# A gated conv and residual quantizer on one core: the first of two sums of conv taps by an accumulating DMA transfer, the second on DVE, and eight of 24 residual updates on DVE

## The chip, the cores and the metric

The kernel runs on one core of one Trainium2 chip. The metric is the device time of one execution in microseconds, lower is better. All runs quoted are of the same ("fast") state, and every comparison is with runs of the kernel before on the same chip in the same rounds.

A core has five engines that run side by side, each in its own instruction order: PE (matmuls), DVE (vector), ACT (scalar), GpSimd (called POOL in the profile) and SP (which here only issues DMA transfers). The order on each engine is fixed when the kernel is built: the scheduler that builds it takes the written program and reorders each engine's instructions within what the data dependences allow. At run time each engine works strictly through that order, so an instruction that waits holds up all those behind it on its engine.

## The reference, cut to what matters

`x` has 2 x 16000 positions of 512 channels (bf16).

```python
z = sum over the 3 taps of xp[:, i:i+T, :] * dw_enc[i]      # depthwise conv, each step rounded to bf16
z = silu(z)                                                 # the gate
res = z
for s in range(4):                                          # four codebooks of 8 entries
    idx = argmin over the 8 entries of the squared distance to res
    q, res = q + cb[idx], res - cb[idx]
y = the same kind of 3-tap conv on q
```

## The kernel before: the parts that matter

The positions are cut into 18 tiles of 1792 (128 rows of 14). For each tile:

- SP issues 14 transposing DMA loads into one of two input buffers `X` (channels on the partitions). GpSimd copies the two halo columns.
- DVE makes three products ("taps") of 128x1792 for each of 4 blocks of channels and adds them up in two rounded sums. ACT and DVE compute the gate from that.
- The quantizer makes chains of small dependent DVE instructions ("decisions": V, KEY, M, OHA and so on, 128x112 elements), each chain closed by PE. 24 residual updates follow: PE computes `pu` into PSUM (the memory that takes PE's results), and either ACT evicts it (after an identity matmul has added the old residual) or DVE adds it. Before, 18 are on ACT and 6 on DVE.
- PE decodes into `py`, ACT copies that to `Y`, and the result is stored.

The tiles overlap in a pipeline: the front of a tile (taps to gate) is worked between the quantizer steps of the tile ahead of it.

```python
def taps(st, i):                                   # once per block of channels, i = 0..3
    X = XT[st["n"] % NX]                           # NX = 2 input buffers
    pk = []
    for k in range(K):                             # three products
        t = ppool.tile([P, R], BF16, name=f"P{k}") # pools of 3 buffers each
        nc.vector.tensor_scalar(out=t, in0=X[:, i, k:k + G, :]..., scalar1=WENC[:, i, k:k + 1], ..., op0=ALU.mult)
        pk.append(t)
    nc.vector.tensor_tensor(out=pk[0], in0=pk[0], in1=pk[1], op=ALU.add)   # first rounded sum
    nc.vector.tensor_tensor(out=pk[0], in0=pk[0], in1=pk[2], op=ALU.add)   # second rounded sum
    nc.scalar.activation(pk[1], pk[0], ACT.Exp, scale=-1.0)

def update(st, s, i, u, on_act):
    ...                                            # PE: pu = [identity @ z if on_act] - codebook @ one-hot
    if on_act: nc.scalar.copy(zg, v)
    else:      nc.vector.tensor_tensor(out=zg, in0=zg, in1=v, op=ALU.add)
# in resid(): update(st, s, i, u, m % 4 != 3)      # m = 0..23
```

## Time and profile before

Time before: 887.77 us, the median of 3 runs (886.93 to 888.55).

| | kernel before |
|---|---|
| repeat of one tile in mid-run | 44.4 us |
| from the start to the first one-hot window copy (`OHW`, 96x896), the fill | 99.7 us |
| from the last such copy to the end, the tail | 50.1 us |
| DVE waits in all | 126 us |

The repeat is read as the distance between the 18 window copies, which come once a tile. The busy line of the page:

```profile
PE 631.2 (71%) x4660; PEld 358.7 (40%) x4711; DVE 739.6 (83%) x1526; ACT 736.1 (83%) x667; POOL 79.7 (9%) x143
```

The windows view, one stretch in mid-run (columns: stretch, its length, busy us of PE, PEld (PE's loading of weights), DVE, ACT and POOL, the clock granted to PE as a share of full speed, DMA share, GB/s):

```profile
500.00:545.00 45.00, 35.65 (x263) 20.01 (x264) 40.45 (x82) 41.19 (x38) 3.80 (x4) 0.92 0.41 84
```

DVE and ACT are both busy for some 40 of 44.4 us a tile. Neither is full, so I read the bound as a loop of DVE, ACT and PE and not as one engine; no run shows this alone, but experiment 6 fits it. What DVE waits for (us in total, times, longest):

```profile
DVE rr L288 <- PE pgr L270: 36.1, 21, 3.3
DVE ZB_139 L386 <- PE pu L380: 27.7, 21, 3.0
DVE ZB_138 L386 <- PE pu L380: 20.2, 19, 3.0
DVE ZB_137 L386 <- PE pu L380: 11.8, 16, 1.5
```

The three `ZB` lines (the updates, 60 us) and `rr` (a reduction of a PE result, 36 us) are all the larger waits of the steady state.

### The profile page before, as it was taken

Reading aid. Unit: us, or ns where it says so; the run is one execution under the profiler, and the core shown is the slowest. Engines: PE = TensorE matmul, PEld = TensorE weight load, DVE = VectorE, ACT = ScalarE, POOL = GpSimd, SP = SyncE. Lnnn points to the kernel's source line nnn. Section 1 sums busy time; section 2 is a strip of 40 time slices with the busy share of each in tenths; the row PEclk is TensorE's granted clock in tenths of the full one; section 3 lists DMA queues with packets and bytes.
Section 4 is the critical chain, followed back from the end, with each engine's and each line's share of the span. In section 5 each row is a group of like instructions: output and inputs, shape, how many; then the busy total and the mean of one; then the engine's idle time right before and its main releaser. Section 6 shows DMA issues by size and latency. Waiting matters only on the chain.

```text
span 888.2 us, 12372 instructions
## 1 busy us (share of the span) xinstructions
PE 631.2 (71%) x4660; PEld 358.7 (40%) x4711; DVE 739.6 (83%) x1526; ACT 736.1 (83%) x667; POOL 79.7 (9%) x143
## 2 busy tenths in 40 slices
PE   1003587878787877777878787878787878778892
PEld 0002253535353535353535353535353535444540
DVE  4499999898989898989898989898989898984731
ACT  0076797989898989898989898989898989997572
POOL 5000000101010101010101010101010100000000
PEclk9998698989898989898989898989898989999997
DMA  4412322343434343434343534333534342020213
GB/s 96 95 30 59 78 46 39 94 74 92 75 94 73 96 71 97 70 100 67 99 68 99 68 97 66 103 65 100 67 99 67 98 69 78 7 84 1 84 51 112
DMA packets 143021, 67.20 MB, mean 76 GB/s; under 512 B 139932, under 2 KB 140572, under 8 KB 140700
## 3 DMA queue, kind: packets, MB, share of 16 engines
q1 hardware_dynamic: 137088, 33.06, 21.7%
q0 software_dynamic: 3840, 32.77, 11.8%
q10 hardware_dynamic: 2032, 0.56, 0.3%
q8 instruction: 37, 0.61, 0.3%
q14 instruction: 24, 0.20, 0.1%
HBM read 0.56 MB, written 32.77 MB: 38 GB/s over the span
## 4 chain that ended last, share of the span: by engine, by line
DVE 39%; ACT 29%; PE 22%; issue 5%; SPq 3%; DMA 1%; ACTq 0%; POOL 0%; POOLq 0%; DVEq 0%
PE pu L380 9%; PE pu L379 7%; ACT ZB_139 L384 6%; ACT ZB_137 L384 5%; ACT Y L402 5%; ACT ZB_138 L384 5%; SPq L228 3%; DVE ZB_137 L255 2%; DVE ZB_138 L255 2%; DVE ZB_139 L255 2%; PE pgr L270 2%; PE py L397 2%; DVE M L324 1%; DVE ZB_138 L386 1%; DVE ZB_139 L386 1%
## 5 line engine op out<-in xcount | busy, mean ns | idle before, releaser
L402 ACT CAST Y<-py 128x1024 bf16<-128x1024 f32 x126 | 130.6, 1043 | 13.8 <-PE py L397 13.8
L384 ACT CAST ZB_138<-pu 128x896 bf16<-128x896 f32 x108 | 95.9, 932 | 18.5 <-PE pu L380 18.0
L384 ACT CAST ZB_139<-pu 128x896 bf16<-128x896 f32 x108 | 95.6, 933 | 17.2 <-PE pu L380 16.7
L384 ACT CAST ZB_137<-pu 128x896 bf16<-128x896 f32 x108 | 95.7, 935 | 10.5 <-PE pu L380 10.5
L379 PEld LDWEIGHTS <-IDENT 128*128 128x128 bf16 x648 | 65.6, 101 | 77.8 <-issue 18.9
L270 PE MATMUL pgr<-ZB_137 128*128 128x152 bf16 (+1 forms) x672 | 56.4, 232 | 50.7 <-DVE ZB_137 L255 47.7
L379 PE MATMUL pu<-ZB_137,IDENT 128*128 128x512 bf16 (+1 forms) x216 | 81.1, 375 | 9.3 <-ACT ZB_137 L384 8.2
L379 PE MATMUL pu<-ZB_138,IDENT 128*128 128x512 bf16 x216 | 80.6, 373 | 7.8 <-ACT ZB_138 L384 6.7
L379 PE MATMUL pu<-ZB_139,IDENT 128*128 128x512 bf16 x216 | 80.1, 371 | 8.3 <-ACT ZB_139 L384 7.0
L267 PE MATMUL pgr<-MSK,IDENT 128*128 128x456 bf16 (+3 forms) x180 | 61.0, 339 | 23.2 <-ACT ZB_137 L384 4.8
L270 PEld LDWEIGHTS <-ZB_137 128*128 128x128 bf16 x672 | 48.4, 101 | 70.3 <-DVE ZB_137 L255 52.3
L288 DVE TENSOR_REDUCE rr<-pgr 128x6 f32<-128x768 f32 (+1 forms) x54 | 41.9, 775 | 36.2 <-PE pgr L270 36.1
L425 POOL DMA_DIRECT2D out_dram<-Y x66 | 34.1, 521 | 389.6 <-ACT Y L402 389.3
L386 DVE TENSOR_TENSOR ZB_139<-ZB_139,pu 128x896 bf16<-128x896 bf16 x36 | 39.1, 1085 | 27.9 <-PE pu L380 27.7
L386 DVE TENSOR_TENSOR ZB_138<-ZB_138,pu 128x896 bf16<-128x896 bf16 x36 | 39.0, 1083 | 20.5 <-PE pu L380 20.2
L270 PE MATMUL pgr<-ZB_139 128*128 128x152 bf16 (+1 forms) x672 | 53.3, 226 | 3.0 <-ACT ZB_139 L384 2.9
L270 PE MATMUL pgr<-ZB_138 128*128 128x152 bf16 (+1 forms) x672 | 53.6, 226 | 2.5 <-ACT ZB_138 L384 2.5
L270 PEld LDWEIGHTS <-ZB_139 128*128 128x128 bf16 x672 | 46.6, 98 | 18.4 <-issue 9.1
L270 PEld LDWEIGHTS <-ZB_138 128*128 128x128 bf16 x672 | 46.6, 98 | 17.7 <-issue 8.9
L386 DVE TENSOR_TENSOR ZB_137<-ZB_137,pu 128x896 bf16<-128x896 bf16 x36 | 39.0, 1084 | 12.1 <-PE pu L380 11.8
L242 ACT ACTIVATE P_348<-P_346 128x1792 bf16<-128x1792 bf16 x1 | 1.7, 1696 | 43.6 <-DVE P_346 L241 43.6
L380 PEld LDWEIGHTS <-CBN_0_262 128*128 128x128 bf16 x144 | 18.9, 131 | 32.6 <-issue 25.3
(1280 smaller groups left out, 1741.0 us busy)
## 6 DMA issues: line engine op xcount, KB each, us to landing
out_dram<-Y POOLq DMA_DIRECT2D x18, 1568.0 KB, 8.5
out_dram<-Y POOLq DMA_DIRECT2D x14, 196.0 KB, 8.2
XT_164<-in_x_dram SPq DMA_TRANSPOSE x126
XT_165<-in_x_dram SPq DMA_TRANSPOSE x126
out_dram<-Y POOLq DMA_DIRECT2D x30, 12.0 KB, 2.1
out_dram<-Y POOLq DMA_DIRECT2D x2, 210.0 KB, 8.9
WDBC<-in_dw_dec_dram ACTq DMA_DIRECT2D x1, 384.0 KB
CB_94<-in_codebooks_dram ACTq DMA_DIRECT2D x16, 8.0 KB
```

The lines of the kernel that those rows point to most:

```text
L228: nc.sync.dma_start_transpose(out=X[:, :, g + 1, :], in_=src[g])
L255: nc.vector.tensor_tensor(out=Z[:, i, :, N3:N3 + P], in0=pk[0].rearrange("p (g c) -> p g c", c=P), in1=pk[1].rearrange("p (g c) -> p g c", ...
L267: nc.tensor.matmul(o, lhsT=IDENT, rhs=MSK[:, 0:nb, c0:c1], start=True, stop=False)
L270: nc.tensor.matmul(o[:, u * w:(u + 1) * w], lhsT=Z[:, i, b0 + u, N3:N3 + P], rhs=Z[:, i, b0 + u, c0:c1], start=False, stop=(u == nb - 1 an ...
L288: nc.vector.tensor_reduce(out=grp(st["rr"], g0, g1)[:, :, :, 0], in_=v[:, :, :, N3:N3 + P], axis=AX.X, op=ALU.max)
L379: nc.tensor.matmul(o, lhsT=IDENT, rhs=zg[:, k0:k0 + nk, :], start=True, stop=False)
L380: nc.tensor.matmul(o, lhsT=CBN[s, u][:, i * P:(i + 1) * P], rhs=W[:, k0:k0 + nk, PADC:PADC + P], start=not on_act, stop=True)
L384: nc.scalar.copy(zg, v)
L386: nc.vector.tensor_tensor(out=zg, in0=zg, in1=v, op=ALU.add)
L397: nc.tensor.matmul(o, lhsT=W[:, k, PADC:PADC + P], rhs=WDEC[u], start=True, stop=not wrap)
L402: nc.scalar.copy(Y[:, 2 * k:2 * k + 2, :].rearrange("p g d -> p (g d)"), py)
L425: nc.gpsimd.dma_start(out=view[p0:p1, lo:hi, :], in_=Y[p0:p1, lo:hi, :])
```

## The change

The intent is to relieve DVE and ACT, the two busiest engines. Half of the rounded sums (72 adds of 1.08 us) leave DVE for the DMA engines: the second product is added into the first by an accumulating transfer. In return DVE takes two more of the 24 updates of each tile from ACT. To make room for the latency, the front is split into steps with positions of their own (`LAG`, in tiles), the pools get their own depths (`NB`), and the stores move to SP and are cut in two. Setup buffers are freed early to make space.

```diff
+    BYDMA = (1,)
+    NB = (5, 3, 4, 3)                       # buffers of P0, P1, P2, E
+    LAG = (0.01, 0.16, 0.31, 0.41, 0.42, 0.60)
...
-            t = ppool.tile([P, R], BF16, name=f"P{k}")
+            t = ppool.tile([P, R], BF16, name=f"P{k}", bufs=NB[k])
...
-        nc.vector.tensor_tensor(out=pk[0], in0=pk[0], in1=pk[1], op=ALU.add)
-        nc.vector.tensor_tensor(out=pk[0], in0=pk[0], in1=pk[2], op=ALU.add)
-        nc.scalar.activation(pk[1], pk[0], ACT.Exp, scale=-1.0)
+    def add(st, i, k):
+        pk = st["pk", i]
+        if k in BYDMA:
+            nc.gpsimd.dma_start(out=pk[0], in_=pk[k], accum_op=ALU.add)
+        else:
+            nc.vector.tensor_tensor(out=pk[0], in0=pk[0], in1=pk[k], op=ALU.add)
+    # expo, plus1, inverse and gate become steps of their own, with a buffer E for the exponential
...
-            nc.gpsimd.dma_start(out=view[p0:p1, lo:hi, :], in_=Y[p0:p1, lo:hi, :])
+            nc.sync.dma_start(out=view[p0:p1, g0 + lo:g0 + hi, :], in_=Y[p0:p1, lo:hi, :])   # in two parts, 8 and 6 rows
...
-                    yield lambda ...: update(st, s, i, u, m % 4 != 3)
+                    yield lambda ...: update(st, s, i, u, (m + 1) * NDVE // 24 == m * NDVE // 24)   # NDVE = 8
...
+        put(n - 1.0, load, st)
+        for i in range(KT):
+            t = n + 0.25 * i
+            put(t, taps, st, i)
+            put(t + LAG[0], add, st, i, 1)      # the transfer
+            put(t + LAG[1], add, st, i, 2)      # the DVE sum that waits for it
+            put(t + LAG[2], expo, st, i)
+            ...
```

More of the change, by code (lines that the diff above doesn't have):

```diff
@@ L51 @@
     const = ctx.enter_context(tc.tile_pool(name="const", bufs=1))
-    ppool = ctx.enter_context(tc.tile_pool(name="ppool", bufs=3))
-    lpool = ctx.enter_context(tc.tile_pool(name="lpool", bufs=2))
-    selp = ctx.enter_context(tc.tile_pool(name="selp", bufs=2))
-    small = ctx.enter_context(tc.tile_pool(name="small", bufs=3))
-    ypool = ctx.enter_context(tc.tile_pool(name="ypool", bufs=2))
+    setup_pool = tc.tile_pool(name="setup", bufs=1)
+    setup = setup_pool.__enter__()
     psA = ctx.enter_context(tc.tile_pool(name="psA", bufs=3, space=bass.MemoryType.PSUM))
@@ L65 @@
     make_identity(nc, IDENT)
-    ONES = const.tile([P, P], BF16, name="ONES")
+    ONES = setup.tile([P, P], BF16, name="ONES")
     nc.vector.memset(ONES, 1.0)
@@ L74 @@
                                 op0=ALU.mult, op1=ALU.add)
-    WENC_b = const.tile([P, KT, K], BF16, name="WENC_b")
-    WDBC = const.tile([P, K, D], BF16, name="WDBC")
-    CB4 = const.tile([P, D], BF16, name="CB4")
-    CB1 = const.tile([NC, D], BF16, name="CB1")
+    WENC_b = setup.tile([P, KT, K], BF16, name="WENC_b")
+    WDBC = setup.tile([P, K, D], BF16, name="WDBC")
+    CB4 = setup.tile([P, D], BF16, name="CB4")
+    CB1 = setup.tile([NC, D], BF16, name="CB1")
     wd_rows = bass.AP(tensor=dw_dec.tensor, offset=dw_dec.offset, ap=[[0, P], [D, K], [1, D]])
@@ L91 @@
     nc.vector.tensor_copy(WENC, WENC_b)
-    CBT = const.tile([P, KT, NC], BF16, name="CBT")
-    CBM2 = const.tile([P, KT, NC], BF16, name="CBM2")
+    CBT = setup.tile([P, KT, NC], BF16, name="CBT")
+    CBM2 = setup.tile([P, KT, NC], BF16, name="CBM2")
     for i in range(KT):
@@ L122 @@
                          start=(i == 0), stop=(i == KT - 1))
-    GR = const.tile([NC, NC], F32, name="GR")
+    GR = setup.tile([NC, NC], F32, name="GR")
     nc.vector.tensor_copy(GR, pg[0:NC, 0:NC])
     NPART = 3
-    GP = const.tile([NC, NPART, NC], BF16, name="GP")
-    GREM = const.tile([NC, NC], F32, name="GREM")
+    GP = setup.tile([NC, NPART, NC], BF16, name="GP")
+    GREM = setup.tile([NC, NC], F32, name="GREM")
     nc.vector.tensor_copy(GP[:, 0, :], GR)
@@ L136 @@
     CCB = const.tile([P, 1, NC], BF16, name="CCB")
-    CCD = const.tile([NC, NPART, NC], BF16, name="CCD")
+    CCD = setup.tile([NC, NPART, NC], BF16, name="CCD")
     nc.vector.tensor_tensor(out=CCD, in0=GP, in1=IDENT[0:NC, 0:NC].rearrange("p (o c) -> p o c", o=1).to_broadcast([NC, NPART, NC]),
@@ L144 @@
     nc.vector.tensor_copy(CCB[:, 0, :], pc[:, 0:NC])
-    GM = const.tile([GC, G, 1], F32, name="GM")
+    GM = setup.tile([GC, G, 1], F32, name="GM")
     nc.vector.tensor_reduce(out=GM[:, :, 0], in_=IDENT[0:GC, 0:GC].rearrange("p (g c) -> p g c", c=C), axis=AX.X, op=ALU.add)
@@ L151 @@
     for s in range(2):
-        SEL = const.tile([NC, G, C], BF16, name=f"SEL{s}")
+        SEL = setup.tile([NC, G, C], BF16, name=f"SEL{s}")
         nc.vector.tensor_copy(SEL, IDENT[0:NC, s * C:(s + 1) * C].rearrange("p (o c) -> p o c", o=1).to_broadcast([NC, G, C]))
-        RP = const.tile([GC, NPART, NC], F32, name=f"RP{s}")
+        RP = setup.tile([GC, NPART, NC], F32, name=f"RP{s}")
         pr = psS.tile([P, 512], F32, name="pr", tag="pss")
@@ L170 @@
     for j in range(4):
-        t = const.tile([P, 1], F32, name=f"JM{j}")
+        t = setup.tile([P, 1], F32, name=f"JM{j}")
         nc.vector.tensor_reduce(out=t, in_=idv[:, :, j, :], axis=AX.XY, op=ALU.add)
@@ L182 @@
                 continue
-            t = const.tile([P, D], BF16, name=f"WJ{j % 2}")
+            t = setup.tile([P, D], BF16, name=f"WJ{j % 2}")
             nc.vector.tensor_scalar(out=t, in0=WDBC[:, k, :], scalar1=JM[j], scalar2=None, op0=ALU.mult)
@@ L211 @@
             nc.gpsimd.memset(k16[:, :, c, 0], c)
+    setup_pool.__exit__(None, None, None)
+    ppool = ctx.enter_context(tc.tile_pool(name="ppool", bufs=3))
+    lpool = ctx.enter_context(tc.tile_pool(name="lpool", bufs=2))
+    selp = ctx.enter_context(tc.tile_pool(name="selp", bufs=2))
+    small = ctx.enter_context(tc.tile_pool(name="small", bufs=3))
+    ypool = ctx.enter_context(tc.tile_pool(name="ypool", bufs=2))
     tiles = []
@@ L239, in taps, with expo, inverse @@
             pk.append(t)
-        nc.vector.tensor_tensor(out=pk[0], in0=pk[0], in1=pk[1], op=ALU.add)
-        nc.vector.tensor_tensor(out=pk[0], in0=pk[0], in1=pk[2], op=ALU.add)
-        nc.scalar.activation(pk[1], pk[0], ACT.Exp, scale=-1.0)
         st["pk", i] = pk
+    def add(st, i, k):
[4 more added lines that the diff above has]
+            nc.vector.tensor_tensor(out=pk[0], in0=pk[0], in1=pk[k], op=ALU.add)
+    def expo(st, i):
+        pk = st["pk", i]
+        E = ppool.tile([P, R], BF16, name="E", bufs=NB[3])
+        nc.scalar.activation(E, pk[0], ACT.Exp, scale=-1.0)
+        st["E", i] = E
     def plus1(st, i):
-        pk = st["pk", i]
-        nc.vector.tensor_scalar(out=pk[1], in0=pk[1], scalar1=1.0, scalar2=None, op0=ALU.add)
+        E = st["E", i]
+        nc.vector.tensor_scalar(out=E, in0=E, scalar1=1.0, scalar2=None, op0=ALU.add)
+    def inverse(st, i):
+        E = st["E", i]
         LN = lpool.tile([P, R], F32, name="LN")
-        nc.scalar.activation(LN, pk[1], ACT.Ln)
-        nc.scalar.activation(pk[1], LN, ACT.Exp, scale=-1.0)
+        nc.scalar.activation(LN, E, ACT.Ln)
+        nc.scalar.activation(E, LN, ACT.Exp, scale=-1.0)
     def gate(st, i):
-        pk = st["pk", i]
         Z = ZB[st["n"] % NZ]
-        nc.vector.tensor_tensor(out=Z[:, i, :, N3:N3 + P], in0=pk[0].rearrange("p (g c) -> p g c", c=P),
-                                in1=pk[1].rearrange("p (g c) -> p g c", c=P), op=ALU.mult)
+        nc.vector.tensor_tensor(out=Z[:, i, :, N3:N3 + P], in0=st["pk", i][0].rearrange("p (g c) -> p g c", c=P),
+                                in1=st["E", i].rearrange("p (g c) -> p g c", c=P), op=ALU.mult)
     def gram(st, g0, g1, c0, c1):
@@ L386, in update @@
             nc.vector.tensor_tensor(out=zg, in0=zg, in1=v, op=ALU.add)
+    NDVE = 8
+    YG = 8
     def decode(st, k):
         W = OHW[st["n"] % NOH]
-        if k == 0:
-            st["Y"] = ypool.tile([P, G, D], BF16, name="Y")
+        if 2 * k % YG == 0:
+            st["Y"] = ypool.tile([P, YG, D], BF16, name="Y")
         Y = st["Y"]
@@ L401, in decode, with store @@
                 nc.tensor.matmul(o, lhsT=W[:, 0, PADC + 1:PADC + 1 + P], rhs=WDEC[3], start=False, stop=True)
-        nc.scalar.copy(Y[:, 2 * k:2 * k + 2, :].rearrange("p g d -> p (g d)"), py)
-        if k == GH - 1:
-            store(st)
-    def store(st):
+        h = 2 * k % YG
+        nc.scalar.copy(Y[:, h:h + 2, :].rearrange("p g d -> p (g d)"), py)
+        if h == YG - 2 or k == GH - 1:
+            store(st, 2 * k - h, 2 * k + 2)
+    def store(st, g0, g1):
         Y, r0, a, e = st["Y"], st["row0"], st["a"], st["e"]
@@ L411, in store @@
         for p in range(P):
-            lo = max(a - G * p, 0)
-            hi = min(e - G * p, G)
+            lo = max(a - G * p, g0) - g0
+            hi = min(e - G * p, g1) - g0
             if lo >= hi:
@@ L424, in store @@
         for p0, p1, lo, hi in split:
-            nc.gpsimd.dma_start(out=view[p0:p1, lo:hi, :], in_=Y[p0:p1, lo:hi, :])
-    def front(st):
-        for j in range(KT + 2):
-            if j < KT:
-                yield lambda j=j: taps(st, j)
-            if 1 <= j <= KT:
-                yield lambda j=j: plus1(st, j - 1)
-            if j >= 2:
-                yield lambda j=j: gate(st, j - 2)
+            nc.sync.dma_start(out=view[p0:p1, g0 + lo:g0 + hi, :], in_=Y[p0:p1, lo:hi, :])
     def select(st):
@@ L450, in resid @@
                 for i in range(KT):
-                    yield lambda s=s, i=i, u=u, m=m: update(st, s, i, u, m % 4 != 3)
+                    yield lambda s=s, i=i, u=u, m=m: update(st, s, i, u, (m + 1) * NDVE // 24 == m * NDVE // 24)
                     m += 1
@@ L464, with put @@
     order = []
+    def put(t, f, *args):
+        order.append((t, len(order), lambda: f(*args)))
     for n, st in enumerate(tiles):
-        order.append((n - 1.0, 0, lambda st=st: load(st)))
-        for off, dur, gen in ((0.0, 1.0, front), (1.05, 0.55, select), (1.6, 1.0, resid), (2.6, 0.8, back)):
+        put(n - 1.0, load, st)
[5 more added lines that the diff above has]
+            put(t + LAG[2], expo, st, i)
+            put(t + LAG[3], plus1, st, i)
+            put(t + LAG[4], inverse, st, i)
+            put(t + LAG[5], gate, st, i)
+        t = n + 0.75 + LAG[5] + 0.05
+        for dur, gen in ((0.55, select), (1.0, resid), (0.8, back)):
             w = list(gen(st))
-            order += [(n + off + dur * (j + 0.5) / len(w), off, f) for j, f in enumerate(w)]
+            for j, f in enumerate(w):
+                put(t + dur * (j + 0.5) / len(w), f)
+            t += dur
     for _, _, f in sorted(order, key=lambda t: t[:2]):
```

## The prediction

> **What bounds it now.** In steady state one tile (18 in all) takes 44.37 us: the chain of waits repeats the same pair of residual evictions at 502.04, 546.41 and 590.78 us. In the windows view a 45 us stretch there has DVE busy 40.6 us, ACT 41.4, PE 35.6. No engine is full; in the chain from 500 to 545 us the first half is ACT evictions and PE updates; from about 522 to 541 us DVE works almost without a gap (decisions, reductions, taps, gates), while ACT thins out.
>
> **What the change does, per tile.**
> - Four of eight DVE adds (1.08 us, 1.0 apart) leave: -4.0 us DVE.
> - Two of 18 ACT evictions (0.93 us, about 0.82 apart) go to DVE (1.085): +2.0 DVE, -1.7 ACT; their four identity matmuls (0.37 each) leave: -1.3 PE.
> - Net: DVE -2.0, ACT -1.7, PE -1.3.
> - Four accumulating transfers of 448 KB come on the GpSimd queue; the stores leave it for SP, cut in two (8 and 6 rows of 14).
> - The instruction order shows taps pulled out of DVE's decision stretch into the ACT-bound one. That relieves 522-541 us, but leaves less filler beside the two corrections, so PE round trips show there.
>
> **The new wait.** The Trainium skill ("DMA: Bandwidth & Descriptors", "SWDGE vs HWDGE vs iDMA") says accumulating needs GpSimd's software descriptors. In the DMA table of before a 12 KB store landed after 2.1 us, a 1568 KB one after 8.5: interpolated, a plain 448 KB copy takes 3.9 us. Accumulating also reads the destination: I estimate 5 to 5.5 us. Between the tap that releases a transfer and the DVE add that needs it stand, in the new order costed with old durations, only 3.4 to 4.8 us. I expect DVE, in order, to wait about 3 us per tile, where it also runs updates that hold PSUM buffers. GpSimd's halo copies stand before a tile's first transfer, but wait for only two transposes.
>
> The skill ("SBUF — State Buffer", "Who interferes with whom") says fast-mode DVE operations and GpSimd's descriptor writing shut each other out. The trace agrees in kind: a tap beside a GpSimd copy took 1.03 us instead of 0.67. I allow 1 us a tile.
>
> **Sum.** About 2 us less work per tile on both leading engines and a better spread (another 2), against some 2.5 of those waits not absorbed: near 42.8 us a tile, -28 us. The final store is under half the size (the last 12 us of before follow the last ACT eviction), -4; a tile's later stages stand 0.35 tile later, +5. I predict **860 us**, 835 to 890 at 8 in 10. Chances: faster by over 2% 0.62, within 2% 0.30, slower 0.08.
>
> **What would show it.**
> - Busy: DVE near 704 us, ACT 706, PE 608; a repeat of 42 to 43.5 us.
> - The add of the third tap waits for the DMA, 40 to 70 us in all; zero means the latency is hidden.
> - The DMA table's landing time, 4 to 6 us.
> - DVE waits for PE at the corrections, near zero before, become 10 to 40 us.
>
> **What would make it wrong.** Accumulating much slower than copying (landing at 8 us would cost over 5 us a tile: slower); transfers starved by transposes, which share the engines; SP holding transposes behind stores. If waits fall where DVE had idle time anyway, a tile could approach 41 us: 835.

## More of the kernel before

DVE waits for an input load just once, for 0.2 us.

In the decisions, two chains are interleaved (timeline of DVE: start, duration, instruction):

```profile
535.68 0.28 DVE L322 TENSOR_TENSOR KEY_288<-V,CCB 128x112 bf16<-128x112 bf16 x1
535.87 0.28 DVE L322 TENSOR_TENSOR KEY_289<-V,CCB 128x112 bf16<-128x112 bf16 x1
536.05 0.26 DVE L324 TENSOR_REDUCE M<-KEY_288 128x14 f32<-128x112 f32 x1
536.23 0.26 DVE L324 TENSOR_REDUCE M<-KEY_289 128x14 f32<-128x112 f32 x1
```

Each instruction starts 0.18 to 0.19 us after the one in front of it, before that one has ended, since the two neighbours do not depend on each other.

## The result

The changed kernel took **1023.68 us** (median of 4 runs, 1022.22 to 1024.97), the kernel before 888.16 us (4 runs, 886.93 to 889.39). The ratio is 1.1525, 95% interval 1.1503 to 1.1548: slower by 15%. Ratios here and below are the mean time of one kernel's fast runs over that of the other's of the same rounds, so not quite the ratio of the medians quoted.

Of the 132 us between the two profiled spans (888.2 and 1020.4), 18 are in the fill (first window copy at 118.0 us instead of 99.7), 120 in the 17 repeats, and the tail is 6 us shorter. Mid-run a repeat takes 54.4 us instead of 44.4; the first and last ones are shorter, and the mean is 50.5 instead of 43.4. The profile after (busy line, one repeat in the windows view, same columns as before):

```profile
PE 671.1 (66%) x4639; PEld 375.2 (37%) x4639; DVE 737.2 (72%) x1490; ACT 710.1 (70%) x631; POOL 110.4 (11%) x149
```

```profile
500.00:554.40 54.40, 38.66 (x257) 21.64 (x256) 40.32 (x79) 39.13 (x36) 5.63 (x6) 0.84 0.45 101
```

ACT did shed 26 us of work. But in a repeat of 54.4 us DVE is busy for only 40.3: it stands idle for 14 us a tile. DVE's waits have doubled, from 126 to 257 us. Summed over the tiles' names from the list of waits:

| DVE waits, us | before | after |
|---|---|---|
| second sum, for the accumulating transfer | none | 83.7 (50 times) |
| taps, for the input load (5 of the 10 labelled with a store, see 2 below) | 0.2 | 32.5 (10 times) |
| `rr`, for PE (first lines of the reductions) | 36.1 | 59.6 |
| updates, for PE | 59.7 | 33.4 |

One repeat of DVE in the timeline (the last column is the idle time in front and what ended it; `P` are products and sums, `XT_152` and `XT_153` the two input buffers):

```profile
496.27 0.68 DVE L244 TENSOR_SCALAR P_4822<-XT_152,WENC 128x1792 bf16<-128x1792 bf16 x1
...
503.01 1.09 DVE L255 TENSOR_TENSOR P_4822<-P_4822,P_4826 128x1792 bf16<-128x1792 bf16 x1 [1.57 <-DMA P_4822<-P_4824]
504.02 1.49 DVE L275 TENSOR_TENSOR ZB_125<-P_4335,E 128x1792 bf16<-128x1792 bf16 x1
...
512.83 1.09 DVE L255 TENSOR_TENSOR P_4985<-P_4985,P_4989 128x1792 bf16<-128x1792 bf16 x1 [2.34 <-DMA P_4985<-P_4987]
...
518.44 0.69 DVE L244 TENSOR_SCALAR P_5474<-XT_152,WENC 128x1792 bf16<-128x1792 bf16 x1 [3.33 <-DMA out_dram<-Y]
...
525.69 0.96 DVE L308 TENSOR_REDUCE rr<-pgr 128x6 f32<-128x768 f32 x1 [3.95 <-PE pgr L290]
...
529.65 0.29 DVE L342 TENSOR_TENSOR KEY_276<-V,CCB 128x112 bf16<-128x112 bf16 x1
529.98 0.27 DVE L344 TENSOR_REDUCE M<-KEY_276 128x14 f32<-128x112 f32 x1
530.28 0.28 DVE L346 TENSOR_TENSOR OHA_268<-KEY_276,M 128x112 bf16<-128x112 f32 x1
...
550.90 0.68 DVE L244 TENSOR_SCALAR P_5307<-XT_153,WENC 128x1792 bf16<-128x1792 bf16 x1
```

And the queue of SP in the same stretch:

```profile
497.01 19.45 SPq L235 DMA_TRANSPOSE XT_152<-in_x_dram  x13
516.56 1.23 SPq L449 DMA_DIRECT2D out_dram<-Y  x3
```

The reader is to see four things.

1. The second sums (L255) wait for their transfers, 1.6 and 2.3 us here.
2. The tap at 496.27 is the last reader of `XT_152`. It ends at 496.95. SP, which waited for that, issues 13 transposes from 497.01 to 516.46. Then DVE's tap at 518.44, the third product of the tile *after next*, waits for this very load. The label of its wait names a store; but the load's last transposes had been issued 2 us earlier, five of the ten waits of this kind are labelled with the load itself and are about as long (2.0 to 3.3 us against 3.3 to 3.8), and in experiment 1 below they all go with the move of one tap. So I take it to be the load. From that tap to the next that frees an input buffer (550.90, ending 551.58) it is 33.1 us. 21.5 us from the freeing to the tap and 33.1 us from there to the next freeing: 54.6 us, the repeat. The load has become a link of a closed loop.
3. In the decisions the dependent instructions now stand alone, 0.30 to 0.33 us apart, with nothing between them; the taps that used to fill the gaps have gone elsewhere.
4. While DVE stands, PE and ACT starve too: ACT's evictions waited 186 us for PE's updates, against 45 before. One of them, in the timeline of ACT:

```profile
521.98 0.91 ACT L404 CAST ZB_126<-pu 128x896 bf16<-128x896 f32 x1 [5.05 <-PE pu L400]
```

The DMA queues (packets, MB, share of the 16 engines' span), the GpSimd queue before and then after:

```profile
q0 software_dynamic: 3840, 32.77, 11.8%
```

```profile
q0 software_dynamic: 10368, 33.03, 18.2%
```

The first carried the stores, the second the 72 transfers of 448 KB. Their median landing time, from issue to landing, was 5.1 us (4.2 to 9.7).

### The profile page after: what moved, and what is told of

It reads as the page before. It is cut to its first block, busy times and chain, and to the rows that moved or that the text cites. A ratio compares the mean times of both kernels' runs of the same rounds, so it can differ in the third digit from the quotient of the medians.

```text
span 1020.4 us, 12437 instructions
## 1 busy us (share of the span) xinstructions
PE 671.1 (66%) x4639; PEld 375.2 (37%) x4639; DVE 737.2 (72%) x1490; ACT 710.1 (70%) x631; POOL 110.4 (11%) x149
## 3 DMA queue, kind: packets, MB, share of 16 engines
q0 software_dynamic: 10368, 33.03, 18.2%
## 5 line engine op out<-in xcount | busy, mean ns | idle before, releaser
L404 ACT CAST ZB_125<-pu 128x896 bf16<-128x896 f32 x96 | 84.6, 915 | 67.4 <-PE pu L400 67.2
L270 ACT ACTIVATE LN<-E 128x1792 f32<-128x1792 bf16 x72 | 123.2, 1712 | 11.7 <-DVE E L265 11.5
L404 ACT CAST ZB_126<-pu 128x896 bf16<-128x896 f32 x96 | 84.9, 917 | 63.3 <-PE pu L400 62.8
L404 ACT CAST ZB_127<-pu 128x896 bf16<-128x896 f32 x96 | 85.1, 918 | 57.1 <-PE pu L400 56.3
L271 ACT ACTIVATE E<-LN 128x1792 bf16<-128x1792 f32 x72 | 122.9, 1712 | 0.1
L399 PEld LDWEIGHTS <-IDENT 128*128 128x128 bf16 x576 | 62.2, 108 | 142.5 <-DVE S L309 66.1
L290 PE MATMUL pgr<-ZB_125 128*128 128x152 bf16 (+1 forms) x672 | 57.8, 240 | 66.1 <-DVE ZB_125 L275 65.9
L399 PE MATMUL pu<-ZB_125,IDENT 128*128 128x512 bf16 x192 | 77.1, 406 | 36.3 <-DVE S L309 23.9
L399 PE MATMUL pu<-ZB_127,IDENT 128*128 128x512 bf16 x192 | 75.3, 396 | 32.1 <-DVE S L309 15.5
L399 PE MATMUL pu<-ZB_126,IDENT 128*128 128x512 bf16 x192 | 75.4, 397 | 29.7 <-DVE S L309 17.7
L308 DVE TENSOR_REDUCE rr<-pgr 128x6 f32<-128x768 f32 (+1 forms) x54 | 41.9, 777 | 59.6 <-PE pgr L290 59.6
L290 PEld LDWEIGHTS <-ZB_125 128*128 128x128 bf16 x672 | 51.2, 105 | 80.7 <-DVE ZB_125 L275 70.1
L287 PE MATMUL pgr<-MSK,IDENT 128*128 128x456 bf16 (+3 forms) x180 | 67.3, 374 | 17.9 <-DVE S L309 9.9
L406 DVE TENSOR_TENSOR ZB_127<-ZB_127,pu 128x896 bf16<-128x896 bf16 x48 | 51.9, 1082 | 19.4 <-PE pu L400 16.3
L290 PE MATMUL pgr<-ZB_126 128*128 128x152 bf16 (+1 forms) x672 | 60.2, 245 | 0.6 <-DVE ZB_126 L406 0.3
L406 DVE TENSOR_TENSOR ZB_126<-ZB_126,pu 128x896 bf16<-128x896 bf16 x48 | 51.9, 1081 | 11.7 <-PE pu L400 10.3
L290 PEld LDWEIGHTS <-ZB_126 128*128 128x128 bf16 x672 | 53.8, 108 | 12.7 <-issue 5.2
L290 PE MATMUL pgr<-ZB_127 128*128 128x152 bf16 (+1 forms) x672 | 57.5, 240 | 0.1
L406 DVE TENSOR_TENSOR ZB_125<-ZB_125,pu 128x896 bf16<-128x896 bf16 x48 | 51.9, 1080 | 7.9 <-PE pu L400 6.8
L290 PEld LDWEIGHTS <-ZB_127 128*128 128x128 bf16 x672 | 52.1, 105 | 12.1 <-issue 4.7
L265 DVE TENSOR_SCALAR E<-E 128x1792 bf16<-128x1792 bf16 x72 | 44.7, 621 | 0.5
```

Of the source, the lines that this page charges most:

```text
L265: nc.vector.tensor_scalar(out=E, in0=E, scalar1=1.0, scalar2=None, op0=ALU.add)
L270: nc.scalar.activation(LN, E, ACT.Ln)
L271: nc.scalar.activation(E, LN, ACT.Exp, scale=-1.0)
L287: nc.tensor.matmul(o, lhsT=IDENT, rhs=MSK[:, 0:nb, c0:c1], start=True, stop=False)
L290: nc.tensor.matmul(o[:, u * w:(u + 1) * w], lhsT=Z[:, i, b0 + u, N3:N3 + P], rhs=Z[:, i, b0 + u, c0:c1], start=False, stop=(u == nb - 1 an ...
L308: nc.vector.tensor_reduce(out=grp(st["rr"], g0, g1)[:, :, :, 0], in_=v[:, :, :, N3:N3 + P], axis=AX.X, op=ALU.max)
```

## The experiments

Theory A: two DMA latencies have entered DVE's in-order stream with too little other work in front of them. One is the input load, which the built order asks for 13 us of DVE work after its buffer is freed (estimate, the instructions in between costed with their durations in the trace before). The other is the transfer, which has only 3.4 to 4.7 us of such work to hide behind and lands after 5.1. Rival B: the transfer is dear in itself (through the DMA engines or through GpSimd, which issues it), wherever it stands. Rival C: the eight updates on DVE, or the split front, did it.

### 1. The input load out of the loop

```diff
-    NB = (5, 3, 4, 3)
+    NB = (5, 3, 3, 3)
```

With three buffers instead of four, the built order moves one tap of each tile: the early third product now comes 39 us of DVE work after its buffer is freed, not 13.

> One number changes: the third tap's product gets 3 buffers instead of 4. In the built DVE order only one instruction moves: the first tap of tile n+2 no longer stands right behind tile n+1's taps, 17 rows after the last tap that reads its X buffer, but a whole decision stretch later. Theory A (a closed loop: last tap frees the X buffer, 13 transposes of about 1.5 us, early tap waits for them, everything behind it on DVE waits too; 22 us of load and 32 us of DVE rows make the repeat of 54.4): DVE's waits for the X load fall from 32 us to under 4, the repeat falls to 48-51 us, the time to 950-985. Rival B (the waits for the accumulating transfers, 84 us, are the cause and the X wait only fills what they leave): the time stays within 1.5% of the changed kernel, 1008-1038, and the accumulate waits grow.

Measured: correct, 974.58 us (972.46 to 976.96), ratio 1.0970 (1.0948 to 1.0992). DVE's waits of this kernel:

```profile
DVE P L255 <- DMA P<-P: 86.4, 52, 9.3
DVE rr L308 <- PE pgr L290: 42.9, 34, 3.7
DVE ZB L406 <- PE pu L400: 33.1, 32, 2.3
```

No tap waits for a load any more; `rr` gives back 17 us too. The move of one instruction is worth 49 us of 135. The wait for the transfers is untouched.

### 2. The transfers into a buffer that nobody reads

Its output is wrong, which doesn't matter for the time. DVE no longer waits for the sum. Not everything else stays, though: compared instruction by instruction in the traces, the built order of DVE, PE and SP is another one, and the transfers, all into one tile, run one after another (GpSimd waited 111 us for the one before). So this is not the changed kernel with one wait taken out.

```diff
-            nc.gpsimd.dma_start(out=pk[0], in_=pk[k], accum_op=ALU.add)
+            nc.gpsimd.dma_start(out=SCR, in_=pk[k], accum_op=ALU.add)     # SCR: one scratch tile
```

> Wrong result on purpose: the accumulating transfers still run, 448 KB each, but into a scratch tile that nobody reads, so no DVE add waits for their landing (the early tap stays, 13 rows behind the freeing tap). Rival B: the 84 us of accumulate waits go and the time falls by 65-90 us, to 935-960. Theory A: the X loop still binds, DVE's waits for the X load grow from 32 us to over 70, the time falls by less than 30 us, to 990-1025.

Measured: 1007.96 us (1006.28 to 1008.73), ratio 1.1342 (1.1325 to 1.1360). The taps' line in the groups of instructions (busy, mean ns, idle in front and its releasers):

```profile
L246 DVE TENSOR_SCALAR P<-XT,WENC 128x1792 bf16<-128x1792 bf16 x216 | 146.3, 710 | 134.7 <-DMA XT<-in_x_dram 88.2 <-DMA SCR<-P 37.2 <-DMA out_dram<-Y 9.0
```

```profile
533.30 18.22 SPq L237 DMA_TRANSPOSE XT<-in_x_dram  x14
551.77 2.59 DVE L246 TENSOR_SCALAR P<-XT,WENC 128x1792 bf16<-128x1792 bf16 x4 [8.63 <-DMA XT<-in_x_dram]
```

84 us of waits were taken away and the time fell by 16, all of it in the fill: the first window copy comes at 99.5 us instead of 118.0, and the 17 repeats together take 861 us against 859. A loop of theory A's kind holds the repeat at 54.6 us without any wait at a sum: 18.5 us from the freeing of the buffer (533.23) to the tap that waits for it, and 36.0 us on to the next freeing. That the length equals the changed kernel's (21.5 and 33.1) is chance. Of the taps' waits, 37 us are labelled with a transfer that still reads the product's buffer; this wait comes back in experiment 10. No single wait's total says what removing it is worth.

### 3. Copies in place of accumulating transfers

Same order, same bytes, no addition. Its output is wrong, which doesn't matter for the time.

```diff
-            nc.gpsimd.dma_start(out=pk[0], in_=pk[k], accum_op=ALU.add)
+            nc.gpsimd.dma_start(out=pk[0], in_=pk[k])
```

> Wrong result on purpose: the transfer copies instead of accumulating; the instruction order on every engine is the same. If accumulating is what is slow (it reads source and destination), the median landing falls from about 5.2 to about 4 us, accumulate waits from 84 to about 40 us and the time by 10-30 us. If the fixed part, descriptor writing and shared engines set the landing, it stays above 4.8 us and the time within 1%.

Measured: 983.05 us (981.67 to 985.31), ratio 1.1067 (1.1046 to 1.1087). The DMA issues and the queue of this kernel:

```profile
P<-P POOLq DMA_DIRECT2D x72, 448.0 KB, 3.2
```

```profile
q0 software_dynamic: 5760, 33.03, 9.7%
```

A copy lands after 3.2 us instead of 5.1, in 5760 packets instead of 10368 and half the queue time; issuing takes GpSimd 0.54 us instead of 0.86. That was worth 40 us, more than I had expected. The waits at the sums fell to 30 us, and the taps' waits for the load grew from 32 to 52. The load's loop still closes, so mid-run the shorter waits at the sums are hardly what shortened it (SP, then DVE):

```profile
475.36 17.43 SPq L235 DMA_TRANSPOSE XT<-in_x_dram  x13
494.81 0.69 DVE L244 TENSOR_SCALAR P<-XT,WENC 128x1792 bf16<-128x1792 bf16 x1 [4.95 <-DMA out_dram<-Y]
```

The 13 transposes were issued in 17.4 us beside copies, instead of 19.5 beside accumulating transfers; in experiment 2, with no transfer in flight, a transpose took 1.30 us, against 1.50 in the changed kernel. The freed buffer was readable after 19.3 us instead of 21.4 (means of six repeats), and the repeat fell from 54.4 to 51.9. So rival B has a part in the changed kernel's own order: the accumulating transfers slow the load beside them. Of the gain, 6.5 us lie in the fill.

### 4. The copies and the load together

The edits of 1 and 3 in one kernel. Its output is wrong, which doesn't matter for the time.

> Wrong result on purpose: the plain copy of the third experiment with the one-buffer edit of the first. If the X wait and the landing time are two causes that add, the gains of the two runs alone (49 and 41 us against the changed kernel) add up to about 90: 925-945. If one hides behind the other, 955-975.

Measured: 926.35 us (925.90 to 928.49), ratio 1.0428 (1.0410 to 1.0445). Together they give back 97 us of the 135; apart 49 and 41. Against experiment 1, with the same order on every engine and the load out of the loop, the copies gained 48 us, and the waits at the sums fell from 86 us to this:

```profile
DVE P L255 <- DMA P<-P: 32.6, 21, 9.1
```

Here the transfer's latency is on DVE's path. The two latencies are both real; that the single gains add up does not show it, since experiment 3 gained mid-run through the load.

### 5. The changed kernel without a transfer

```diff
-    BYDMA = (1,)
+    BYDMA = ()
```

> Both sums on DVE again (4.0 us a tile of DVE work back), all else of the change kept. Theories A and B both expect it to return most of the loss: 880-905. Rival C (what costs is that the new order took the filler out of DVE's decision stretch and put the stores in front of the loads, whatever does the sum): it stays above 930.

Measured: correct, 893.79 us (890.77 to 896.94), ratio 1.0060 (1.0029 to 1.0091). With all sums back on DVE, the split front, the pools, the moved stores and the eight updates are within 1% of the kernel before. Rival C falls: nearly all of the 135 us hang on the transfers being there, directly or through the order that the build chose with them.

### 6. The kernel before with eight updates on DVE

```diff
-                    yield lambda ...: update(st, s, i, u, m % 4 != 3)
+                    yield lambda ...: update(st, s, i, u, (m + 1) * 8 // 24 == m * 8 // 24)
```

> The kernel before with only the other half of the change: eight of 24 residual updates on DVE instead of six. ACT loses 1.7 us a tile, PE 1.3, DVE gains 2.0. As DVE sets the decision stretch and ACT the rest: within 2% of before, 875-900.

Measured: correct, 893.92 us (892.55 to 894.63), ratio 1.0067 (1.0052 to 1.0082). ACT falls to 704 us and DVE rises to 769, and the repeat stays at 44.4 us. This part of the change brings nothing alone.

### 7 to 9. DVE in the written order: three runs that told little

I wanted to separate the scheduler's order from the waits by making DVE follow the program as written.

```diff
-    for _, _, f in sorted(order, key=lambda t: t[:2]):
-        f()
+    with tc.manual_schedule(engines={mybir.EngineType.DVE}):
+        for _, _, f in sorted(order, key=lambda t: t[:2]):
+            f()
```

Number 7 is the changed kernel with this edit:

> The changed kernel with one edit: DVE issues its instructions in the order in which the kernel's loop writes them, not in the order that the building scheduler made of it (the other engines stay scheduled). No tap then stands early: from a last tap that frees an X buffer to the next tap that reads it are some 60 rows instead of 17. Between releasing tap and waiting add stand 5.9, 8.8, 4.1 and 3.1 us of DVE work (old durations) instead of 3.9, 4.7, 3.6 and 3.4. Theory A: waits for X under 4 us, accumulate waits 84 -> 40-60 us, repeat 46-49 us, time 905-950. If it was the transfer traffic or the stores on SP that cost, the order does not help: above 970.

Number 8 also puts the waiting sum a quarter of a tile behind its transfer, `LAG = (0.01, 0.26, 0.38, 0.47, 0.48, 0.64)`:

> As the run before it, and the second add and all behind it written later (lag 0.26 of a tile instead of 0.16): 6.9 to 14.2 us of DVE work between releasing tap and waiting add, more than the 5.1 us landing. Theory A (both DMA waits are what the change cost): accumulate waits under 12 us, X waits under 4, and the gain in work shows: repeat 42-44.5 us, time 845-890. Rival C (the moved filler and PE round trips cost as much as the work saved): above 900 with the DMA waits gone.

Number 9 is the control, the kernel before with this edit:

> Control for the written order: the kernel before with DVE in the written order. Its two adds stand right behind the taps, so nothing waits for a DMA. Expected within 4% of before, 880-925; were it much faster than before, a gain of the two runs with written order would belong to the order and not to the change.

Measured: 1075.55 us (ratio 1.2123), 1017.88 us (1.1464) and 1117.9 us (1.2592), all correct. The control decides how to read them: the written order costs 26% in the kernel that has no transfer at all, so it is a poor background for this question. In number 8 the waits for the transfers fell to 24 us from 79 and those for loads are zero, yet the updates waited 107 us for PE. All three are misses of what I expected, the control too (880 to 925). All that can be kept is that number 8 is 5% below number 7 for the longer lag.

### 10. Hold the waiting sum back

With the scheduler's order kept otherwise, an edge of order alone (no wait at run time) forbids the waiting sum to stand before the update written last before it, and the pool of experiment 1 keeps the load out of the loop.

```diff
-    NB = (5, 3, 4, 3)
+    NB = (5, 3, 3, 3)
...
-            nc.vector.tensor_tensor(out=pk[0], in0=pk[0], in1=pk[k], op=ALU.add)
+            a = nc.vector.tensor_tensor(out=pk[0], in0=pk[0], in1=pk[k], op=ALU.add)
+            if "update" in last: <a may not be placed before last["update"], the last residual update on DVE>
```

In the built order 23 to 33 us of DVE work now stand between a transfer's tap and its sum (estimate as above), and taps are back among the decisions.

> The changed kernel with the third tap's product in 3 buffers (as in the first experiment) and one ordering edge: the DVE add that waits for the transfer may not be issued before the residual update on DVE that the loop wrote last before it. The scheduler still orders the rest. In the built order 23 to 33 us of DVE work (old durations) now stand between releasing tap and waiting add, 34 us between the tap that frees an X buffer and the next that reads it, and adds, taps and gates stand between the steps of the decision stretch again. Theory (two exposed DMA waits plus the lost filler make the whole loss; the transfers as such cost nothing): accumulate waits under 5 us, X waits under 5, repeat 41.5-44 us, time 840-880, faster than before. Rival (the traffic, GpSimd's descriptor writing, or stores on SP cost by themselves): at or above 900 with the waits gone.

Measured: correct, 914.14 us (909.61 to 916.63), ratio 1.0295 (1.0273 to 1.0317). The number was missed, the repeat was not: it is 43.9 us, below the 44.4 of the kernel before. What is lost lies in the fill (first window copy at 118.5 us) and in a new wait:

```profile
DVE P L245 <- DMA P<-P: 62.1, 32, 11.3
DVE ZB L410 <- PE pu L404: 44.0, 43, 2.6
DVE P L256 <- DMA P<-P: 16.0, 6, 9.2
```

The sums (L256) wait for 16 us instead of 84 (under 5 expected). Now the taps (L245) wait 62 us: a product's buffer is not free until the transfer that reads it has landed, and with three buffers the next tap wants it too soon.

### 11. No transfer in the first two tiles

On top of 10:

```diff
-        if k in BYDMA:
+        if k in BYDMA and st["n"] >= 2:
...
-            if "update" in last:
+            if k == 2 and st["n"] >= 2 and "update" in last:
```

> The kernel that holds the waiting sums, with the sums of the first two tiles of positions wholly on DVE (no transfer while the pipeline fills); every later tile as before. If the transfers' latency at the start is what made the fill long (first one-hot window copy at 118.5 us against 99.7 in the kernel before), that copy comes back to 98-104 us, the repeat stays near 44 us, and the time falls from 914 us to 880-898 us. Rival: the fill is long because of the order in which the work is written (it starts the taps of later tiles too early), not because of the transfers: then the first copy stays at 112 us or later and the time is over 905 us.

Measured: correct, 889.63 us (888.38 to 891.00), ratio 1.0010 (0.9986 to 1.0033). The first window copy is back at 100.7 us and the repeat stays at 43.9. So the longer fill came from the transfers' latency while the pipeline was empty; the rival is out. (The edit also frees these tiles' sums from the edge of experiment 10. Experiments 2 and 5, without that edge and without waits at the sums for a transfer, have the first copy at 99.5 and 100.1 us.) The taps still waited 54 us for buffers.

### 12. Keep the taps of a tile together as well

On top of 11, a tap may not be placed before the third gate of the tile before (order alone), so that the first and second products of a block are made next to each other and the transfer starts at once; P0 gets 7 buffers, since the sums now live longer.

```diff
-    NB = (5, 3, 3, 3)
+    NB = (7, 3, 3, 3)
...
-            nc.vector.tensor_scalar(out=t, in0=X[...], ...)
+            m = nc.vector.tensor_scalar(out=t, in0=X[...], ...)
+            if n > 0: <m may not be placed before the gate of block 2 of tile n - 1>
```

> As the run beside it, and the taps of a tile are placed behind the third gate of the tile before (an edge of order alone), so that a first-tap and a second-tap product are made next to each other and no buffer is held long for a transfer; the pool of first-tap products has 7 buffers instead of 5. Theory: the 62 us of DVE waits for product buffers held by transfers (in the kernel that holds the sums) fall under 25 us, the repeat falls from 44 to 42-43.5 us, and the total is 850-885 us, below both kernels. Rival: the wait is only moved to the sums or to ACT and PE, since the repeat of 44 us is already set by the rest of the loop: then the repeat stays at 43.8-45 us and the total is 880-905 us.

Measured: correct, **858.63 us** (857.56 to 859.10), ratio 0.9663 (0.9639 to 0.9686), below both kernels. The busy line and one repeat in the windows view:

```profile
PE 604.2 (71%) x4588; PEld 347.6 (41%) x4639; DVE 726.7 (85%) x1498; ACT 708.1 (83%) x631; POOL 107.7 (13%) x141
```

```profile
500.00:541.90 41.90, 32.48 (x255) 18.84 (x257) 39.10 (x79) 39.08 (x36) 5.48 (x6) 0.96 0.64 132
```

DVE's waits:

```profile
DVE ZB L413 <- PE pu L407: 36.9, 37, 3.1
DVE ZB L282 <- ACT E L278: 14.9, 17, 1.0
DVE rr L315 <- PE pgr L297: 14.3, 21, 3.1
...
DVE P L245 <- DMA P<-P: 3.9, 1, 3.9
```

One wait of 3.9 us is all that is left of the transfers, no sum waits, and no tap waits for a load. Between a transfer's tap and its sum stand 10 to 30 us of DVE work (estimate). DVE idles 2.8 us of a 41.9 us repeat, where the changed kernel idled 14. Against the profile before, the 17 repeats are worth 25.7 us, the tail 5.8 and the fill 0.9: the 32.4 us between the spans of 888.2 and 855.8.

### 13. The same without a transfer

Is that gain the transfers' or only the order's?

```diff
-    BYDMA = (1,)
+    BYDMA = ()
```

> The version that holds the sums and the taps (858.6 us), with no transfer: the first sums are back on DVE (64 sums of 1.09 us, 70 us of DVE time, 4 us for each of 16 tiles). If the transfers' saved DVE time is what makes that version faster than the kernel before, this one takes 885-925 us. Rival: the order alone made the gain, and the transfers are worth little: then it takes under 870 us.

Measured: correct, 874.98 us (873.43 to 876.12), ratio 0.9840 (0.9821 to 0.9859). This fell between the two expectations. The build also orders some DVE instructions differently here, so the split is approximate: of about 30 us, about 14 come with the rest of the version (its tail is 6.5 us shorter than before's, its repeats together 7.7) and about 16 with the transfers. Those took 53 us of busy time from DVE (779.7 to 726.7), of which under a third reached the total.

### 14. The same with copies

12 with the edit of 3, in the very same order on all engines. Its output is wrong, which doesn't matter for the time.

> Wrong on purpose: the same version in the same order, the transfers copy instead of adding (landing 3.2 us instead of 4.6-5.1, half the packets, GpSimd 0.54 us instead of 0.86). In the changed kernel's own order this took 40 us off. Theory: with 10 us and more of other DVE work between a transfer's issue and the sum that reads it, its length is off the loop: 852-862 us, within 1% of 858.6. Rival: the transfers still cost through GpSimd, the port or the queues: then it is under 845 us.

Measured: 856.94 us (854.67 to 858.94), ratio 0.9635 (0.9608 to 0.9662). The landing time falls from 4.6 to 3.0 us and the total by 0.2%, within the scatter. The same exchange took 40 us off the changed kernel. With enough work in front of the sum, neither the addition nor the transfer's length, nor GpSimd's part, is on the loop. Rival B, dear wherever it stands, falls, since 12 is also faster than 13; what is left of it is the slowed load of experiment 3, in an order where the load is in the loop.

## Why the prediction was wrong

The prediction was 860 us, faster with 0.62; the result was 1023.68 us, far outside the range of 835 to 890.

- **Right: the work removed from ACT, and the tail.** ACT 710 us (predicted 706), the tail 6 us shorter (4).
- **Right: the transfer's length.** "I estimate 5 to 5.5 us"; it landed after 5.1. "Between the tap that releases a transfer and the DVE add that needs it stand ... only 3.4 to 4.8 us": that was the order that ran.
- **Right in kind, short in size: the waits at the second sum.** 40 to 70 us expected, 83.7 measured.
- **Wrong: the search for load waits stopped at GpSimd.** "GpSimd's halo copies stand before a tile's first transfer, but wait for only two transposes." The same new order was not read for who *else* asks for the load early. DVE's third product of the tile after next stood 13 us of work behind the tap that frees its buffer, and the load takes 21.5 us from that freeing. That put the load into a closed loop of 54.6 us. Experiment 1 moves that one tap and gains 49 us; experiment 2, in a somewhat other order, shows such a loop holding the repeat with no wait at a sum left.
- **Wrong: "a better spread (another 2)".** Taking the taps out of the decisions was entered as a gain of 2 us a tile, with a doubt beside it ("less filler"). By the trace, though not by an experiment, the doubt was the larger term. Alone, dependent small instructions come 0.30 to 0.33 us apart, where two interleaved chains start one every 0.18, and `rr` waited 24 us more for PE. (The prediction looked for this at the two corrections, 10 to 40 us; there DVE waited for PE for 4.4 us at most.) Part of this shows as busy time: DVE was busy for 737 us, not the predicted 704, while experiment 10, with the same 1490 DVE instructions and the filler back, was busy for 706.6. Counted from its start to the start of the next, the 770 small instructions make 21 of these 31 us. I did not move the filler alone, so its own share of the total is not settled.
- **Wrong: "some 2.5 of those waits not absorbed" as the whole price.** A wait in an in-order stream was priced by its own length. DVE also runs the updates that free PSUM for PE; while it waited, ACT waited for PE four times as long as before (186 us against 45). With the load out of the loop, shortening the transfer by 2.0 us, 72 times, is 141 us of landing time and gained 48 (experiment 4 against 1), so there the waits were on the loop. In the changed kernel's own order the load's loop covers them mid-run (experiments 2 and 3).
- **Short: the fill.** All that was allowed is "a tile's later stages stand 0.35 tile later, +5"; it took 18 us more to the first window copy, since nothing is there yet to hide a transfer behind. In the order of experiment 10, experiment 11 takes these back by leaving the first two tiles on DVE; close to the changed kernel's own order, experiment 2 does, where no sum waits for a transfer.
- **Not foreseen: PE.** It was busy for 671 us, not 608. Its identity matmuls for the updates took 0.40 us each instead of 0.37, at a mean granted clock of 0.88 instead of 0.92 (experiment 12: 604 us, 0.37 and 0.94). The lower clock goes with this kernel in all four of its runs; whether it cost time of its own is not separated.

The estimate of the gain was not absurd: with an order that hides the transfers the same idea took 858.63 us. What failed was the belief that the built order offers that. Of the 38 us that are left after experiment 4 (926 against 888), 11 lie in the fill and 34 in the repeats, and the tail is 6 shorter; 33 us of waits for the copies and the missing filler are in them, and I have not taken them apart further.

## What to carry to other kernels

When work is handed to a DMA transfer, look in the built order for two distances on the in-order engine: from the transfer's issue to its first reader, and from each buffer's last reader to the next instruction that needs what is loaded into it; both must hold more other work than the transfer lasts. A wait's total in the profile is no bound on what it costs or on what its removal gains, because the next wait of the same loop takes over; move one instruction or one pool depth to see which loop sets the repeat, and look whether the built order stayed otherwise the same, as it did not in experiment 2. Here the same transfers cost 15% with 4 us of work in front of their readers and brought 3.4%, with the rest of that version, with 10 to 30 us; the Trainium skill ("DMA: Bandwidth & Descriptors", "Rules for kernel authors") gives the same advice, to issue early, compute, and wait late, and experiments 12 and 14 agree with it.

## What the Trainium skill lacked or had wrong

- "DMA: Bandwidth & Descriptors", "Anatomy of one DMA — SWDGE (gpsimd) path" fits a transfer as about 2.0 us and bytes over 436e3, which gives an estimate of 3.05 us for 448 KB. The plain copy took 3.0 to 3.2 us here, which agrees. The page gives no figure for an accumulating transfer: 4.6 to 5.1 us for the same bytes, 10368 packets instead of 5760, 18.2% of the queue time instead of 9.7%, and 0.86 us of GpSimd to issue instead of 0.54.
- The same page gives rates for transposing loads but no time for a load made of many: here 13 transposes took SP 19.45 us to issue, 1.5 us each, so that a freed input buffer was readable only 21.5 us later. Beside copies the 13 took 17.4 us; with no transfer in flight a transpose took 1.30 us.
- "VectorE: DVE Perf Modes", "The DRAIN you can't avoid" reports that eight copies took the same time with a semaphore after each as with one after the last. What is lacking is a figure for small dependent instructions (128x112), another case than these copies: here 0.30 to 0.33 us from start to start in a bare chain, 0.18 to 0.19 where two independent chains are interleaved.
- "SBUF — State Buffer", "Who interferes with whom" says that a DVE instruction with two inputs in SBUF contends with a GpSimd instruction that reads SBUF. The trace agrees, with a size that the page lacks: the gate at 504.02 took 1.49 us, beside a GpSimd copy that ran from 503.39 to 504.57; so did ten more of the 72 gates, each beside such a copy, and the others took about 1.08.
